# Attention opening and loop ordered by one table for four engines, attention outputs normalised per token

## The chip, the cores and the metric

The kernel runs on one core of one Trainium2 chip. Time is device time in microseconds (us), the median of the runs made. The engines speak of themselves as in the profile: PE is the matrix engine (PEld its weight loads), DVE the vector engine, ACT the scalar engine, POOL GpSimd; SP only issues transfers.

## The reference

Two batches of 768 tokens, 8 heads of 64: attention with 8 global and 96 local keys, then a dense feed-forward layer with a Mish gate over 1536 tokens, then a mixture of 8 experts with one expert per token.

```python
scores = scale * np.matmul(q, k.transpose(0, 1, 3, 2)) + bias      # bias: -slope * distance
a = np.exp(np.where(keep, scores, -1e9) - max)
attn = np.matmul(a / (a.sum(-1) + 1e-9), v)                        # 12 tiles of 128 tokens
h = x @ w_in                                                       # 1536x512 @ 512x2048, float64 weights
x = (h * tanh(softplus(h))) @ w_out                                # 2048x512
expert = argmax(x @ w_gate); out = gate * (relu(x @ w1[expert]) @ w2[expert])
```

## The kernel before

Attention is done tile by tile (12 tiles of 128 tokens), each in two steps of four heads (24 steps `s`). A step is: `a_S` scores on PE into PSUM; `a_max` (DVE, one instruction per head: bias added and row maximum); `a_exp` (ACT, with the row sum); `a_T` transposes of the probabilities on PE; `a_Tev` copies of them to SBUF (ACT); `a_V` the product with v on PE. After both steps of a tile, before the change, `a_recip` inverts the sums and spreads them over 512 columns on DVE (L324), `a_R` transposes that on PE (L330), `a_Rc` copies it to SBUF on ACT (L335), and `a_xm` multiplies the outputs, which stand with features on the partitions, by it. `a_xh` and `a_xl` split the result in a rounded part and a remainder.

The feed-forward layer is cut into 48 units (three passes over the weights, 6 blocks of 256 tokens): per unit `L1_mms` is 24 matmuls of 256 columns (L441), `L2_mms` 12 of 512 columns (L460), two units later; between them stands the Mish chain of 11 parts (0, 2, 3, 4 and 9 on ACT, the others on DVE, L468 to L500). The weights come as 64-bit floats in 32 chunks; each is converted by `next_conv(0)`, three DVE instructions (L168, L170, L172), `next_conv(1)`, one on ACT (L206), and `next_conv(2)`, one on DVE (L208). 16 chunks serve the first two passes, units 0 to 23; the other 16 are first used by unit 24.

The first 10 units (0 to 9) are woven into the attention steps. Only the opening (up to step 4) stands under a manual schedule there; the loop after it is written in Python order, and the framework's scheduler decides where on each engine an instruction stands. It pulled instructions of the code behind the loop, conversions above all, into the loop. What follows the loop, units 10 to 47, the routing and the experts, is written the same in both kernels. Transfers are issued by SP in one order. `prefill` writes zero rows to the gather buffer with 24 transfers, all at unit 16.

In the opening, `fill` issues matmuls of the identity that compute nothing needed; `make_ints` turns the two integer inputs, loaded to all 128 partitions, into floats; the bias tiles `ndist` are built from them on DVE in ten instructions a part (`bias_part`, L113 to L122); `prep_qk` scales a tile's q in one instruction (DVE for tile 0, POOL for the others, L267).

Of the kernel before, what the change touches and what calls it, by code (L numbers as in the profile page):

```python
# [8 lines left out]
F32 = mybir.dt.float32  # L9
# [25 lines left out]
NWARM = 17  # L35
# [7 lines left out]
def moe_kernel(ctx, tc, q, k, v, n_global, n_local, w_in, w_out, w_gate, w1, w2, out, dbg=None):  # L43
# [17 lines left out]
    int_raw = const.tile([128, 2, 2], I32, name="int_raw")  # L61
    for i_, src_ in enumerate((n_local, n_global)):
        nc.scalar.dma_start(int_raw[:, i_, :], src_.bitcast(I32).unsqueeze(0).broadcast_to([128, 2]))
# [4 lines left out]
    def make_ints():  # L68
        f = const.tile([128, 2, 2], F32, name="int_f")
        nc.vector.tensor_copy(f, int_raw)  # L70
        neg = const.tile([128, 2], F32, name="int_n")
        nc.vector.tensor_single_scalar(neg, f[:, :, 0], 0.0, op=ALU.is_lt)
        nc.vector.tensor_add(neg, neg, f[:, :, 1])
        nc.vector.scalar_tensor_tensor(out=nlg, in0=neg, scalar=4294967296.0, in1=f[:, :, 0],
                                       op0=ALU.mult, op1=ALU.add)

# [181 lines left out]
    def prep_qk(t):  # L258
# [6 lines left out]
        eng = nc.vector if t == 0 else nc.gpsimd  # L265
        with tc.issue_after(gorder[0]) if t > 2 else nullcontext():
            eng.tensor_tensor(out=qkt[t], in0=qkt[t], in1=qsc.unsqueeze(2).to_broadcast([128, 4, 128]), op=ALU.mult)  # L267
# [15 lines left out]
    rbs = {}  # L283
# [35 lines left out]
    def a_recip(t):  # L319
        su = rcs.pop(t)  # L320
        nc.vector.tensor_scalar_add(su, su, 1e-9)
        nc.vector.reciprocal(su, su)
        sp_ = xe.tile([128, ROW], F32, tag="x2", name="sp_")[:, 0:DM]
        nc.vector.tensor_copy(sp_.rearrange("p (a b) -> p a b", b=64), su.unsqueeze(2).to_broadcast([128, H, 64]))  # L324
        rbs[t] = sp_

    def a_R(t):
        rb = ps.tile([128, 4, 128], F32, tag="b", name="rb")
        for p_ in range(4):
            nc.tensor.transpose(rb[:, p_, :], rbs[t][:, p_ * 128:p_ * 128 + 128], ident)  # L330
        rbs[t] = rb

    def a_Rc(t):
        rs = xe.tile([128, ROW], F32, tag="x2", name="rs")[:, 0:DM].rearrange("p (a b) -> p a b", a=4)
        nc.scalar.copy(rs, rbs[t])  # L335
        rbs[t] = rs

# [26 lines left out]
    def a_V(s):  # L364
# [4 lines left out]
        if pr == 0:  # L369
            av_ps[t] = ps.tile([128, 4, 128], F32, tag="b", name="av")  # L370
        av = av_ps[t]
        va = vv[0:nk, 0]
        vb = vv[:, 1]
        for i in range(2):
            for c in range(2):
                for j in range(2):
                    q_ = 2 * i + j
                    h = 4 * pr + q_
                    hs = slice(h * 64, h * 64 + 64)
                    lh = va[:, hs] if c == 0 else vb[:, hs]  # L380
                    rh = PT[0:nk, 0, q_, :] if c == 0 else PT[:, 1, q_, :]
                    nc.tensor.matmul(av[64 * j:64 * j + 64, 2 * pr + i, :], lhsT=lh, rhs=rh,
                                     start=(c == 0), stop=(c == 1))
# [3 lines left out]
    def a_xm(t):  # L387
# [4 lines left out]
        xm = rbs.pop(t)  # L392
        nc.vector.tensor_mul(xm, av_ps.pop(t), xm)
        return xm

    def a_xh(t, xm):
        blk, o = divmod(t, 2)
        nc.scalar.copy(xT[blk][0][:, :, o * 128:o * 128 + 128], xm)  # L398

    def a_xl(t, xm):  # L400
# [3 lines left out]
        ins = nc.vector.tensor_sub(xl[:, :, cs], xm, xh[:, :, cs].bitcast(F32)).ins  # L404
# [7 lines left out]
        return ins  # L412

    def a_x(t):
        xm = a_xm(t)
        a_xh(t, xm)
        return a_xl(t, xm)
# [96 lines left out]

    def acc_evac(u):
        p, b, j = units[u]
        ac = accs.pop(b)
        for o in range(2):
# [8 lines left out]
            else:  # L527
                if p == 0:
                    xp = xe.tile([128, DM], F32, tag="xp", name="xpo", bufs=4)
                    nc.scalar.copy(xp, ac[o])  # L530
                else:
                    xp = xpl[b][o]
                    nc.vector.tensor_add(xp, ac[o], xp)
# [76 lines left out]
    def prefill():  # L610
# [9 lines left out]
    pass  # L620
# [233 lines left out]
    NS = 5  # L854
    with tc.manual_schedule(engines={mybir.EngineType.PE, mybir.EngineType.Activation, mybir.EngineType.DVE, mybir.EngineType.Pool}), tc.tile_pool(name="tmp0", bufs=1, side="right") as tmp0:
# [8 lines left out]

        fill(NWARM)
        ci = tmp0.tile([128, NG], I32, name="ci")
# [3 lines left out]
        next_raw()  # L870
        load_v(1)
        load_qk(2)
        next_raw()
        next_raw()
        def some(it, n_):
            for _ in range(n_):
                next(it, None)

        def heads(f, s_, qs=range(4)):
            for q_ in qs:  # L880
                f(s_, q_)
# [8 lines left out]
        make_ints()  # L890
        nc.vector.tensor_scalar(out=gk, in0=cf, scalar1=ng, scalar2=None, op0=ALU.is_lt)
        some(b0, 4)
        prep_qk(0)
        some(b0, 5)
        a_S(0)
        a_S(1)
        prep_qk(1)
        bias_diag(ndist)
        heads(a_max, 0)
        heads(a_exp, 0)  # L900
        heads(a_max, 1)
        some(b1, 11)
        bias_copies(ndist)
        fill(4)
        a_T(0, 0)
        a_T(0, 1)
        heads(a_exp, 1)
        a_S(2)
        a_Tev(0, 0)
        a_Tev(0, 1)  # L910
        a_T(1, 0)
# [529 lines left out]
```

## Time and profile before

| | |
|---|---|
| runs | 603.31, 601.72, 603.13 us; median 603.13 |
| profiled execution | 601.62 us; its span from first to last instruction 599.8 us |
| busy share of the span | PE 96%, PEld 86%, DVE 80%, ACT 63%, POOL 15% |
| granted TensorE clock | 0.996 on average |
| moved by DMA | 109.97 MB, mean 183 GB/s |

Times in the rows below are from the start of the span. The attention part lasts to 156.9 us, where unit 10, the first one behind the loop, starts on PE. A busy time joins the overlapping spans of an engine's instructions: an instruction of 0.69 us can be followed by the next one after 0.60 us, so the distance of two starts is what an instruction costs its engine.

### The profile page before, as it was taken

How to read it: one execution, taken by the hardware profiler on the slowest of the kernel's cores; microseconds unless marked ns; L12 is line 12 of the kernel's file. 1: busy time of each engine (PE TensorE's matmuls, PEld its weight loads, DVE VectorE, ACT ScalarE, POOL GpSimd, SP SyncE). 2: the span in 40 equal slices, each digit the busy share in tenths (PEclk: the TensorE clock that was granted, in tenths of full speed). 3: DMA queues.
4: the chain of work that ended last, by engine and by line, in shares of the span. 5: the costliest groups of instructions: out<-in, count | busy, mean ns of one | idle time of the engine just before them, and what ended most of it. 6: DMA issues, size and time to landing. Idle time of an engine off the chain costs nothing.

```text
span 599.8 us, 11918 instructions
## 1 busy us (share of the span) xinstructions
PE 575.7 (96%) x4288; PEld 518.5 (86%) x4288; DVE 480.0 (80%) x1151; ACT 378.7 (63%) x882; POOL 88.4 (15%) x157
## 2 busy tenths in 40 slices
PE   8988999999999999999999999989999999999994
PEld 7766777777889899898989889779999999999994
DVE  5999999999699899776867667655985678888942
ACT  3898788898676565656455555465664566776731
POOL 3211210000110010010210301121201212113111
PEclk9999999999999999999999999999999999999998
DMA  7976555756899856322221310367667284586200
GB/s 225 343 246 190 179 209 172 241 191 229 282 304 300 326 187 227 113 71 80 98 89 54 106 36 36 114 251 281 203 243 251 96 310 164 199 307 235 106 18 22
DMA packets 54935, 109.97 MB, mean 183 GB/s; under 512 B 5723, under 2 KB 12891, under 8 KB 54866
## 3 DMA queue, kind: packets, MB, share of 16 engines
q1 hardware_dynamic: 48882, 90.21, 45.0%
q0 software_dynamic: 5696, 18.89, 9.6%
q8 instruction: 36, 0.59, 0.4%
q14 instruction: 33, 0.27, 0.1%
q10 hardware_dynamic: 288, 0.00, 0.0%
HBM read 84.67 MB, written 25.10 MB: 183 GB/s over the span
## 4 chain that ended last, share of the span: by engine, by line
PE 66%; DVE 15%; ACT 11%; DMA 5%; issue 2%; SPq 0%; POOL 0%; DVEq 0%; ACTq 0%; POOLq 0%
PE hp L441 18%; PE acc L460 16%; PE bacc L724 6%; PE bhp L724 6%; ACT P L316 3%; PE bacc L725 3%; PE bhp L725 3%; DVE P L305 2%; ACT PT L362 2%; DVE bw L158 2%; PE bhp L727 1%; PE bacc L727 1%; PE bacc L729 1%; PE bacc L728 1%; PE bhp L728 1%
## 5 line engine op out<-in xcount | busy, mean ns | idle before, releaser
L460 PE MATMUL acc<-wpair,gh 128*128 128x512 f32 x384 | 123.8, 400 | 1.4 <-ACT gh L497 1.4
L441 PE MATMUL hp<-xh,wpair 128*128 128x256 f32 x768 | 121.0, 287 | 2.3 <-ACT xh L398 2.2
L441 PEld LDWEIGHTS hp<-xh,wpair 128*128 128x128 f32 x768 | 104.3, 188 | 9.8 <-ACT xh L398 4.2
L460 PEld LDWEIGHTS acc<-wpair,gh 128*128 128x128 f32 x384 | 68.1, 188 | 16.5 <-issue 1.9
L158 DVE TENSOR_TENSOR bw<-bst,bw 128x512 fp32r<-128x512 f32 x112 | 72.9, 685 | 9.7 <-ACT bw L157 8.9
L157 ACT CAST bw<-bst 128x512 fp32r<-128x512 f32 x112 | 64.5, 620 | 19.6 <-PE bhp L728 9.8
L460 PE MATMUL acc<-wpair,gl 128*128 128x512 f32 x192 | 75.4, 393 | 0.8 <-DVE gl L500 0.8
L468 ACT ACTIVATE e<-hp 128x512 f32<-128x512 f32 x48 | 28.7, 598 | 71.3 <-PE hp L441 71.3
L441 PE MATMUL hp<-xl,wpair 128*128 128x256 f32 x384 | 63.9, 284 | 0.3 <-DVE xl L404 0.3
L724 PE MATMUL bhp<-xc,bw 128*128 128x352 f32 (+4 forms) x192 | 59.3, 364 | 0.7 <-DVE t L759 0.6
L724 PE MATMUL bacc<-hc,bw 128*128 128x352 f32 (+4 forms) x192 | 59.2, 364 | 0.0
L316 ACT ACTIVATE P<-P,mx 128x232 f32<-128x232 f32 (+1 forms) x96 | 44.7, 470 | 15.1 <-DVE mx L305 15.0
L441 PEld LDWEIGHTS hp<-xl,wpair 128*128 128x128 f32 x384 | 52.8, 188 | 1.0 <-DVE xl L404 0.9
L725 PE MATMUL bhp<-xc,bw 128*128 128x176 f32 (+4 forms) x192 | 48.5, 253 | 0.0
L725 PE MATMUL bacc<-hc,bw 128*128 128x176 f32 (+4 forms) x192 | 48.3, 252 | 0.0
L478 DVE SCALAR_TENSOR_TENSOR n<-n,r 128x512 f32<-128x512 f32 x48 | 33.1, 689 | 16.7 <-ACT r L476 15.9
L460 PEld LDWEIGHTS acc<-wpair,gl 128*128 128x128 f32 x192 | 36.1, 188 | 8.8 <-DVE gl L500 1.3
L500 DVE SCALAR_TENSOR_TENSOR gl<-n,gh 128x512 fp32r<-128x512 f32 x48 | 33.0, 688 | 11.6 <-ACT gh L497 10.6
L497 ACT ACTIVATE gh<-n 128x512 fp32r<-128x512 f32 x48 | 30.1, 628 | 13.4 <-DVE n L493 13.2
L472 ACT ACTIVATE n<-e 128x512 f32<-128x512 f32 x48 | 30.3, 632 | 13.1 <-DVE e L470 13.0
L724 PEld LDWEIGHTS bhp<-xc,bw 128*128 128x128 f32 x192 | 36.1, 188 | 1.7 <-DVE t L759 0.8
L423 POOL DMA_DIRECT2D xl<-xs x12 | 6.9, 576 | 204.9 <-PE hp L441 137.1
(220 smaller groups left out, 1278.2 us busy)
## 6 DMA issues: line engine op xcount, KB each, us to landing
bst<-in_moe_w_dram SPq DMA_DIRECT2D x56, 512.0 KB
wst<-in_moe_w_in_dram SPq DMA_DIRECT2D x16, 512.0 KB
wst<-in_moe_w_out_dram SPq DMA_DIRECT2D x16, 512.0 KB
xl<-xs POOLq DMA_DIRECT2D x12, 512.0 KB, 4.0
xh<-xs POOLq DMA_DIRECT2D x12, 512.0 KB, 4.9
xpl<-xps SPq DMA_DIRECT2D x24, 256.0 KB
xg<-z SPq DMA_DIRECT2D x24, 224.9 KB
w0f<-in_moe_w_dram SPq DMA_DIRECT2D x8, 512.0 KB
```

The source lines that it names most:

```text
L157: nc.scalar.copy(hi, src)
L158: nc.vector.tensor_sub(lo, src, hi.bitcast(F32))
L316: nc.scalar.activation(out=Ps[s][:, q_, 0:w], in_=Ps[s][:, q_, 0:w], func=AF.Exp, bias=mxs[s][:, q_:q_ + 1], scale=-1.0, accum_out=rcs[t][ ...
L441: yield lambda f=f, kk=kk, wi=wi, xx=xx, cs=cs: nc.tensor.matmul(hp[:, f, :], lhsT=w[:, wi, kk, cs], rhs=xx[:, kk, :], start=(kk == 0 and ...
L460: yield lambda f=f, o=o, cs=cs, gi=gi, wi=wi, first=first, last=last: nc.tensor.matmul(accs[b][o], lhsT=gi[:, cs], rhs=w[:, wi, f, :], sta ...
L468: nc.scalar.activation(out=e, in_=hp, func=AF.Exp, scale=-1.0)
L472: nc.scalar.activation(out=n, in_=e, func=AF.Square)
L478: nc.vector.scalar_tensor_tensor(out=n, in0=n, scalar=0.25, in1=r, op0=ALU.add, op1=ALU.mult)
L497: nc.scalar.mul(gts[u][0], n, -(2.0 ** -80))
L500: nc.vector.scalar_tensor_tensor(out=gl, in0=n, scalar=-(2.0 ** -80), in1=gh.bitcast(F32), op0=ALU.mult, op1=ALU.subtract)
L724: nc.tensor.matmul(o[:, 0:2 * cap], lhsT=wh, rhs=xc, start=first, stop=False)
L725: nc.tensor.matmul(o[:, 0:cap], lhsT=wl, rhs=xh, start=False, stop=last)
```

## The change

Opening and loop now stand in one table, `ORDER`, of 666 operations, all under the manual schedule for PE, ACT, DVE and POOL: each engine runs its instructions in the order of the table. The letters are the functions above (S scores, M maximum, E exponential, T and C transposes and their copies, V product with v, R, N, X, h, l the end of a tile, L and G four matmuls of `L1_mms` and three of `L2_mms`, m a part of the Mish chain, c, d, e the three parts of a conversion, v the copy of a finished partial sum).

`a_V` swaps its operands: the probabilities are the weights, v streams, and the output has tokens on the partitions. Each of the 8 matmuls of 128 columns in a step becomes two of 64. The inverted sums are then one factor per partition and head: one DVE instruction per tile (`a_n`) reads the PSUM output and applies them, four transposes (`a_X`) bring features to the partitions, and `a_xh`, `a_xl` read those from PSUM. The spread, its transposes and its copy fall away. The integers are loaded to one partition and spread by a matmul with ones; q of tiles 0 and 1 is scaled on ACT in eight pieces; 17 and 4 filling matmuls become 6 and 3; the 24 zero-row transfers are spread over units 14 to 21, three each. The Mish chain of unit 9 is finished inside the table.

```diff
-NWARM = 17
+NWARM = 6
+LOOPU = 10
...
-    int_raw = const.tile([128, 2, 2], I32, name="int_raw")
+    int_raw = const.tile([1, 2, 2], I32, name="int_raw")
...
+        nc.tensor.matmul(warm[:, 0:2], lhsT=one, rhs=z, start=True, stop=True)
+        nc.vector.tensor_copy(nlg, warm[:, 0:2])
...
+    def scale_q(s):
+        t, pr = divmod(s, 2)
+        for p_ in (2 * pr, 2 * pr + 1):
+            nc.scalar.mul(qkt[t][:, p_, :], qkt[t][:, p_, :], qsc[:, p_:p_ + 1])
...
-                    nc.tensor.matmul(av[64 * j:64 * j + 64, 2 * pr + i, :], lhsT=lh, rhs=rh,
-                                     start=(c == 0), stop=(c == 1))
+            for c in (1, 0):
+                n = nk if c == 0 else 128
+                for j in range(2):
+                    r = slice(64 * j, 64 * j + 64)
+                    nc.tensor.matmul(av_ps[t][r, h, :], lhsT=PT[0:n, c, q_, r], rhs=vv[0:n, c, h * D:h * D + D],
+                                     start=(c == 1), stop=(c == 0))
...
+    def a_n(t):
+        xns[t] = xe.tile([128, ROW], F32, tag="x2", name="xn")[:, 0:DM]
+        nc.vector.tensor_tensor(out=xns[t].rearrange("p (a b) -> p a b", b=D), in0=av_ps.pop(t),
+                                in1=rcs.pop(t).unsqueeze(2).to_broadcast([128, H, D]), op=ALU.mult)
+
+    def a_X(t):
+        xn = xns.pop(t)
+        xps_[t] = ps.tile([128, 4, 128], F32, tag="b", name="xp")
+        for p_ in range(4):
+            nc.tensor.transpose(xps_[t][:, p_, :], xn[:, p_ * 128:p_ * 128 + 128], ident)
...
+    ORDER = """
+    q0 b0 q1 S0 S1 M0.0 q2 M1.0 M1.1 E0.0 M0.1 S2 M0.2 E1.0 M0.3 M1.2 E0.1 M1.3 b1 E0.2 E0.3 b2 E1.1 T0.0 E1.2 c0
...
+    m9.9 l11 v2.0 G7 v2.1 m10.9 G7 e13 v3.0 v3.1
+    """.split()
...
+        for tok in ORDER:
+            ACT_[tok[0]](*tok[1:].split("."))
...
-        if u == 16:
-            prefill()
+        if 14 <= u < 22:
+            for _ in range(CAPMAX // 112):
+                next(zero_rows, None)
```

On PE, one place in the loop: before, a step's scores (`sp`), transposes (`pt`), the product with v (`av`) and the transposed sums (`rb`).

```order
L292 MATMUL sp<-kT,qr 128x232 x4
L347 MATMUL pt<-ident,P 104x128 x4
L349 MATMUL pt<-ident,P 128x128 x4
L382 MATMUL av<-PT,vv 64x128 x8
L330 MATMUL rb<-ident,sp__566 128x128 x4
```

The same engine now, behind the scores of tile 1 (`xp` is the transposed output of a tile).

```order
L301 MATMUL sp<-kT,qr 128x232 x8
L337 MATMUL pt<-ident,P 104x128 x4
L339 MATMUL pt<-ident,P 128x128 x4
L337 MATMUL pt<-ident,P 104x128 x4
L339 MATMUL pt<-ident,P 128x128 x4
L385 MATMUL xp<-ident,xn 128x128 x4
L367 MATMUL av<-vv,PT 64x64 x32
```

A step's product with v is 16 matmuls of 64 columns where it was 8 of 128 (the 32 are two steps); the four transposes a tile stand on its output in place of its sums.

On DVE, the rows from the remainder of the last tile (`xl`) on, before: 22 conversions (`cv<-wst`) of 32 have been started up to here, eight of them from the code behind the loop.

```order
L404 TENSOR_TENSOR xl<-rs,xh 128x4x128
L482 TENSOR_TENSOR e<-e,r 128x512
L493 TENSOR_TENSOR n<-e,hp 128x512
L500 SCALAR_TENSOR_TENSOR gl<-n,gh 128x512
L470 TENSOR_SCALAR e<-e 128x512
L208 TENSOR_TENSOR wpair_0_2480<-cv,wpair_0_2480 128x512 x2
L168 TENSOR_SCALAR cv<-wst 128x512 x2
L170 SCALAR_TENSOR_TENSOR cv<-wst,cv 128x512
L478 SCALAR_TENSOR_TENSOR n<-n,r 128x512
```

The same place now; the second `gl` row ends the chain of unit 9.

```order
L398 TENSOR_TENSOR xl<-xp,xh 128x4x128
L488 SCALAR_TENSOR_TENSOR gl<-n,gh 128x512
L211 TENSOR_TENSOR wpair_0_1866<-cv,wpair_0_1866 128x512
L173 SCALAR_TENSOR_TENSOR cv<-wst,cv 128x512
L171 TENSOR_SCALAR cv<-wst 128x512
L175 SCALAR_TENSOR_TENSOR cv<-wst,cv 128x512
L173 SCALAR_TENSOR_TENSOR cv<-wst,cv 128x512
L175 SCALAR_TENSOR_TENSOR cv<-wst,cv 128x512
L458 TENSOR_SCALAR e<-e 128x512
L211 TENSOR_TENSOR wpair_2_2290<-cv,wpair_2_2290 128x512
```

The table holds 14 conversions, and the scheduler draws two more ahead of this place, so that 16 have been started here where it was 22 (15 against 22 are through their three instructions, 14 against 20 through the last one). From the `gl` of unit 9 to that of unit 23, the last unit that needs none of the later weights, DVE's order holds 165 instructions on 512 columns, 31 of them with one tensor operand (`TENSOR_SCALAR`), 134 with two.

On SP, the zero rows (`xg<-z`) before, in nearly one piece:

```order
L618 DMA xg<-z 112x514 x9
L534 DMA xps<-xpo 128x512 x2
L512 DMA xpl<-xps 128x512 x2
L618 DMA xg<-z 112x514 x12
L534 DMA xps<-xpo 128x512 x2
L618 DMA xg<-z 112x514
L182 DMA wst<-in_moe_w_in_dram 128x2x512
```

and now:

```order
L614 DMA xg<-z 112x514 x3
L185 DMA wst<-in_moe_w_in_dram 128x2x512
L507 DMA xps<-xpo 128x512 x2
L500 DMA xpl<-xps 128x512 x2
L185 DMA wst<-in_moe_w_in_dram 128x2x512
L190 DMA wst<-in_moe_w_out_dram 128x1024
L507 DMA xps<-xpo 128x512 x2
L614 DMA xg<-z 112x514 x2
```

They stand in groups of at most three; before, four weight chunks (`wst`) stand behind the first of them, now eight.

## Rows read from the trace of the kernel before

**Rows 1.** Windows: busy us of PE, PEld, DVE, ACT, POOL, clock, DMA share, GB/s.

```profile
0.00:10.80 10.80, 8.47 (x54) 8.18 (x55) 5.55 (x28) 1.28 (x1) 3.99 (x26) 1.00 0.68 197
15.00:150.00 135.00, 127.61 (x1072) 101.48 (x1070) 131.60 (x384) 114.47 (x314) 13.82 (x20) 1.00 0.67 222
0.00:156.90 156.90, 146.24 (x1194) 117.15 (x1194) 143.64 (x440) 124.57 (x342) 21.07 (x55) 1.00 0.68 222
156.90:237.30 80.40, 79.56 (x506) 72.03 (x507) 75.38 (x135) 50.31 (x86) 7.76 (x14) 1.00 0.87 272
```

**Rows 2.** The chain that ended last: start us, us, what.

```profile
156.91 0.74 PE hp L441 x4
...
162.83 2.88 PE hp L441 x24
165.71 2.76 PE acc L460 x12
...
245.86 2.76 PE acc L460 x12
```

**Rows 3.** Timeline of the opening: start us, us, engine, line, instruction, wait before it.

```profile
1.67 6.89 PE L863 MATMUL warm<-ident 128*128 128x128 f32 x34 [1.67 <-POOL ident masks.py:199]
...
6.74 0.17 DVE L70 CAST int_f<-int_raw 128x4 f32<-128x4 int32 x1 [3.61 <-DMA int_raw<-in_n_global_dram]
...
8.44 0.68 DVE L267 TENSOR_TENSOR qr<-qr,qsc 128x512 f32<-128x512 f32 x1
...
8.76 1.26 POOL L267 TENSOR_TENSOR qr<-qr,qsc 128x512 f32<-128x512 f32 x1 [3.24 <-DMA qr<-in_q_dram]
9.04 1.07 DVE L119 TENSOR_SCALAR loc<-loc 128x136 f32<-128x136 f32 x1
...
10.81 0.30 DVE L305 CUSTOM_DVE_ANT_0 P<-sp,ndist 128x136 f32<-128x136 f32 x1 [0.15 <-DVE ndist L122]
...
13.30 0.21 DVE L119 TENSOR_SCALAR loc<-loc 128x104 f32<-128x104 f32 x1
```

**Rows 4.** Timeline of PE inside the loop.

```profile
124.73 1.05 PE L292 MATMUL sp<-kT,qr 64*128 64x232 f32 x8
125.71 0.74 PE L460 MATMUL acc<-wpair,gh 128*128 128x512 f32 x2
...
126.52 0.60 PE L347 MATMUL pt<-ident,P 128*104 128x128 f32 x4
126.96 0.60 PE L349 MATMUL pt<-ident,P 128*128 128x128 f32 x4
...
128.32 0.60 PE L330 MATMUL rb<-ident,sp__1685 128*128 128x128 f32 x4
128.85 1.10 PE L382 MATMUL av<-PT,vv 104*64 104x128 f32 x16
129.88 0.50 PE L460 MATMUL acc<-wpair,gh 128*128 128x512 f32 x1
```

**Rows 5.** Windows of line L382 alone: busy of PE and PEld.

```profile
0.00:156.90 156.90, 28.62 (x384) 20.33 (x384) 1.00 0.68 222
```

**Rows 6.** The chain again, the routing's logits.

```profile
277.63 1.04 PE lp L555 x32
```

**Rows 7.** Windows of line L324 alone: busy of DVE.

```profile
0.00:156.90 156.90, 6.13 (x12) 1.00 0.68 222
```

**Rows 8.** Timeline of DVE behind the loop.

```profile
188.01 0.69 DVE L208 TENSOR_TENSOR wpair<-cv,wpair 128x512 fp32r<-128x512 f32 x1
188.61 0.69 DVE L482 TENSOR_TENSOR e<-e,r 128x512 f32<-128x512 f32 x1
189.22 0.42 DVE L470 TENSOR_SCALAR e<-e 128x512 f32<-128x512 f32 x1
189.55 0.69 DVE L493 TENSOR_TENSOR n<-e,hp 128x512 f32<-128x512 f32 x1
```

**Rows 9.** Waits, 160 to 215 us: who waited for what, us in total, times, longest.

```profile
DVE cv L168 <- DMA wst<-in_moe_w_in_dram: 1.7, 1, 1.7
```

More of the change, by code (lines that the diff above doesn't have):

```diff
@@ L317, in a_exp @@
                              bias=mxs[s][:, q_:q_ + 1], scale=-1.0, accum_out=rcs[t][:, h:h + 1])
[L319 to L336, printed above, removed]
     pts = {}
@@ L513, in part_load, with evac0 @@
             xpl[b].append(xp)
+    def evac0(b, o):
+        t = 2 * b + o
+        xp = xe.tile([128, DM], F32, tag="xp", name="xpo", bufs=4)
+        nc.scalar.copy(xp, accs[b][o])
+        nc.sync.dma_start(xps[t * 128:(t + 1) * 128, :], xp)
+        if o == 1:
+            del accs[b]
     def acc_evac(u):
         p, b, j = units[u]
+        if p == 0:
+            evac0(b, 0)
+            evac0(b, 1)
+            return
         ac = accs.pop(b)
@@ L527, in acc_evac @@
             else:
[L528 to L533, printed above, removed]
+                xp = xpl[b][o]
+                nc.vector.tensor_add(xp, ac[o], xp)
                 nc.sync.dma_start(xps[t * 128:(t + 1) * 128, :], xp)
@@ L618, in prefill @@
                 tc.keep_in_program_order(nc.sync.dma_start(xg[r0:r0 + 112, :], z))
-    pass
+                yield
+    zero_rows = prefill()
     cnt = const.tile([1, NE], F32, name="cnt")
@@ L865, in moe_kernel @@
         fill(NWARM)
+        wi = ps.tile([128, 512], F32, tag="b", name="wi")
+        one = tmp0.tile([128, 128], F32, name="one")
+        z = tmp0.tile([128, 2], F32, name="z")
+        nc.vector.memset(one, 1.0)
+        nc.vector.memset(z, 0.0)
         ci = tmp0.tile([128, NG], I32, name="ci")
@@ L889, in moe_kernel @@
         some(b1, 2)
-        make_ints()
+        make_ints(z, one, wi)
+        fill(3)
         nc.vector.tensor_scalar(out=gk, in0=cf, scalar1=ng, scalar2=None, op0=ALU.is_lt)
-        some(b0, 4)
         prep_qk(0)
[L894 to L906, printed above, removed]
@@ L1050, in moe_kernel, with bias, v_end, scores @@
-    u0 = u
+        def bias(part):
+            some({"0": b0, "1": b1, "2": b1}[part], 4 if part == "1" else 11)
+            if part == "0":
+                bias_diag(ndist)
+            if part == "2":
+                bias_copies(ndist)
+        l1 = [L1_mms(u) for u in range(LOOPU)]
+        l2 = [L2_mms(u) for u in range(LOOPU)]
+        def v_end(s):
+            a_V(s)
+            if s % 2 and s // 2 + 2 < NTILE:
+                load_v(s // 2 + 2)
+        def scores(s):
+            a_S(s)
+            if s % 4 == 3 and 1 < s // 2 // 2 + 2 + 0 < NTILE // 2 and s > 3:
+                load_qk(2 * (s // 4) + 4)
@@ new lines, in half1, with consts @@
+        def half1(c):
+            next_conv(0)
+            next_raw()
+        def consts(_):
+            make_fast()
+            build_consts(tmp0)
+        ACT_ = {
+            "b": lambda a: bias(a), "q": lambda s: scale_q(int(s)), "p": lambda t: prep_qk(int(t)),
+            "S": lambda s: scores(int(s)), "V": lambda s: v_end(int(s)), "R": lambda t: a_rec(int(t)),
+            "N": lambda t: a_n(int(t)), "X": lambda t: a_X(int(t)), "h": lambda t: a_xh(int(t)),
+            "l": lambda t: a_xl(int(t)), "c": half1, "d": lambda c: next_conv(1), "e": lambda c: next_conv(2),
+            "k": consts,
+            "M": lambda s, q_: a_max(int(s), int(q_)), "E": lambda s, q_: a_exp(int(s), int(q_)),
+            "T": lambda s, c: a_T(int(s), int(c)), "C": lambda s, c: a_Tev(int(s), int(c)),
+            "L": lambda u: run_mms(l1[int(u)], 4), "G": lambda u: run_mms(l2[int(u)], 3),
+            "m": lambda n, u: mish(int(u), int(n)), "v": lambda b, o: evac0(int(b), int(o)),
+        }
@@ L1079, in phase_, with chain @@
         run_mms(it, 99)
+    def chain(u, *parts):
+        if 0 <= u < NU:
+            for q_ in parts:
+                mish(u, q_)
     for u in range(u0, NU + 2):
@@ L1110, in moe_kernel @@
             next_conv(1)
-        chain(u - 1, 10)
+        chain(prev, 10)
         for _ in range(nch):
```

233 lines of the change are left out of this document (52 added, 181 removed).

## The prediction

> **What bounds the kernel now.** I read the windows first. Inside the loop (15 to 150 us) DVE is busy 131.60 of 135 us, 97%, ACT 114.47 (85%), PE 127.61 [rows 1]. PE's 95% deceives, because the end of a matmul is modelled: a distance of starts says more. Its timeline gives 0.98 us for a score step (124.73 to 125.71), 0.44 for four transposes (126.52 to 126.96), 1.03 for a product with v (128.85 to 129.88), 0.53 for the four transposes of the sums (128.32 to 128.85) [rows 4]; the chain gives 2.88 us for an L1 and 2.76 for an L2 [rows 2]. So PE's need up to unit 10 is 24 x (0.98 + 2 x 0.44 + 1.03) = 69.4, 12 x 0.53 = 6.4, 10 x 2.88 = 28.8 and 8 x 2.76 = 22.1: 126.7 us. It had from the end of the filling matmuls at 8.56 [rows 3] to 156.91 [rows 2], 148.3 us, and was really at work for 85%. DVE bounds the attention part, and PE waits for it in small pieces.
>
> Behind the loop PE is the bound: from 156.91, where unit 10's L1 starts, to 245.86, where unit 23's L2 starts [rows 2], stand 16 L1 and 15 L2, 16 x 2.88 + 15 x 2.76 = 87.5 us of work in 88.95. But DVE has little left there too: 75.38 of 80.40 us [rows 1].
>
> **The change, part by part.**
>
> *Sums applied per token, DVE.* The 12 spreads vanish: 6.13 us [rows 7]. The multiplication stays one instruction per tile with a PSUM operand, and so does `xl`; I cost both as before (0.60 us from start to start [rows 8]). No row shows an operand that is repeated 64 times from one column; if it ran twice as long, the price is 12 x 0.6 = 7 us of DVE.
>
> *PE.* The transposes change places, 12 x 4 before and after. The product with v keeps its streamed columns but doubles the weight loads, to 32 per step in the trace's count (16 instructions, two passes each). The nearest row is the routing's logits: 32 matmuls with 64 weight columns each, in two halves of the array, 1.04 us [rows 6], against 1.03 for today's product. They stream only 8 columns, so this bounds from below: it shows that such loads follow each other at 0.033 us. From above: today's loads are busy 20.33 us for 384 [rows 5], 0.053 us each; if these stand one behind the other, a step takes 32 x 0.053 = 1.69 us, and PE gains 24 x 0.66 = 15.8 us. I take the lower value, since the logits have the same shape of weights and the same alternation of halves. The Trainium skill (TensorE: Matmul & The Clock Gate, section "LDWEIGHTS (loading the stationary operand)") speaks against the change here: a load costs its columns divided by 1.2 ns, 53 ns for 64 columns, 1.71 us a step. By that PE's need would be 143 us instead of 126.7; the logits' row does not bear it out for alternating halves.
>
> *Conversions leave the loop.* At the last `xl` DVE has 14 two-operand instructions and 6 one-operand ones of conversions fewer, and 6 of their subtractions: 20 x 0.60 + 6 x 0.33 = 14.0 us [rows 8]. With the spreads, the q scaling (0.68 [rows 3]) and two chain instructions more (1.2), DVE's 143.64 us up to 156.9 [rows 1] become about 143.6 - 14.0 - 6.1 - 0.7 + 1.2 = 124. ACT loses 12 copies and some conversions and gains eight short scalings; it stays under its 124.57 us. So three engines now need 124, under 124 and 126.7 us: PE, by a little, is the one that the table has to keep busy.
>
> *Opening.* The first maximum stands at 10.81 us. DVE waits 3.61 us for the integers, to 6.74; then the scaling of q, 0.68, stands in its way, and L119 takes 1.07 us while POOL's own scaling runs from 8.76, where the narrower one at 13.30 takes 0.21 [rows 3]. Both scalings leave: about 1.5 us earlier. One descriptor for each integer in place of 128 should come earlier, the matmul and copy behind it cost something; no row shows either: I bound it by -1 and +2 us and take +1. Together 2.5 us, so the table starts at 8.3 and PE's scores at about 8.2. Tile 1's q lands only at 8.76 [rows 3], and ACT's first exponential now stands behind its scaling, which holds ACT's part of the gain to about 2 us.
>
> *Fewer filling matmuls.* The granted clock is shown as 1.00 for 0 to 10.8 us [rows 1], but 34 matmuls of 128 columns took 6.89 us, 0.20 each [rows 3], where the loop's 128-column transposes take 0.11 [rows 4]: most of them ran at the lower level of 1.2 GHz, and PE was busy without a break until the speed doubled. With 12 of them, a wait, and 8 more, the rise may come later; if it comes 6 us later, with PE busy half that time, 3 us are lost, partly under DVE's and ACT's first work. I take 1.5 us, between 0 and 5. By the Trainium skill (the same page, Part 1, "The HAM clock gate") the lower level is the default and only activity lifts it, which bears in the same direction.
>
> *Where unit 10 starts.* DVE as the bound of the old loop reached 97% [rows 1]. I give PE the same: 8.2 + 126.7 / 0.97 + 1.5 = 140.3 us, against 156.9. With no wait at all it is 134.9; at 93%, 145.9.
>
> *What is given back behind the loop.* DVE's order from unit 9's `gl` to unit 23's has 165 instructions: 134 x 0.60 + 31 x 0.33 = 90.6 us, with 2% for waits 92.5, against PE's 87.5. DVE starts on it about 1 us ahead of unit 10's L1. So DVE becomes the bound there, and unit 23's L2 starts 91.5 us after unit 10's L1, at 231.8, where it was 245.86. Past it DVE has no conversions left, and the instructions are the same in both kernels: the 14.1 us stay to the end. Spreading the zero rows moves no byte away; eight weight chunks now stand among them on SP's queue where four did. One such wait cost 1.7 us before [rows 9]; I count none, and price it as a rival.
>
> *The sum.* 601.62 - 14.1 = 587.5 for a run like the profiled one, which lies 1.5 us below the median of the three; I predict 588 us.
>
> **The rivals.**
> 1. Better: the table runs without waits, the clock rises as early as before, and DVE's 90.6 us behind the loop are hidden to the last 2 us: unit 10 at 135, unit 23's L2 at 135 + 89.5 = 224.5, 21 us gained, 580. For it: in its best stretch behind the loop PE was busy 79.56 of 80.40 [rows 1]. Against it: three engines that are all filled above 90% and each held to a fixed order wait for each other.
> 2. Weight loads that don't overlap: PE needs 142.5 us, unit 10 at 8.2 + 142.5 / 0.97 + 1.5 = 156.6, no sooner than before, and DVE's 91.5 then end at 248: 604, slower by 2. It decides when a step of `av` passes about 1.6 us.
> 3. The order itself stalls, and this ends on the slower side: an instruction at the head of one engine's queue waits for a value that the table's author expected earlier, and everything behind it on that engine waits as well, which the old loop's scheduler avoided by pulling other work forward. If PE is at work for no more than 85%, as now, unit 10 starts at 8.2 + 149.1 + 1.5 = 158.8, and with the longer DVE list behind it unit 23's L2 at 250.3, 4.4 us late: 606. It decides at 88%: there nothing is gained.
> 4. Weights late: from 156.9 to 237.3 the DMA share was 0.87 at 272 GB/s [rows 1], and the same bytes plus four chunks must pass in less time. Three waits of the size of the one seen cost 5 us: 592.
>
> **How the numbers follow.** The forecast, 588 with 583 to 592 as its own range (PE at 95 to 99% of its time in the table), has a chance of 0.48; rival 1 0.14, rival 2 0.08, rival 3 0.12, rival 4 0.18. The range of 578 to 599 takes in the forecast, rivals 1 and 4, and leaves out 2 and 3, two in ten. A difference of 0.3%, 1.8 us, is about what a measurement of this kernel can tell from none. Faster by more than that hold the forecast, rivals 1 and 4 and the milder cases of 3: 0.83; the same 0.06; slower 0.11.
>
> **What would show it.** In the profile after: the first maximum at 8 to 9 us; a step of `av` with 32 matmuls at 1.0 to 1.1 us from start to start; no L324, L335; DVE under 95% and PE's real work over 93% up to unit 10's L1, which starts at 136 to 145 us; from there to unit 23's L2 90 to 94 us, with PE waiting for `gl` and DVE nearly full. It would be wrong if `av` costs 1.6 us or more, if the stretch behind the loop keeps 88 us, or if the loop shows waits of PE on ACT or DVE that add up to more than 15 us.

## The result, and the profile after

The changed kernel took 586.71 us (median of four runs, 586.55 to 590.01); the kernel before, on the same chip, 603.22 us (601.72 to 606.16). The ratio is 0.9733, with a 95% interval of 0.9683 to 0.9784: 16.5 us faster. The profiled execution took 586.55 us, with a span of 584.8 us where it had been 599.8.

The page after, engines' busy time in the whole span:

```profile
span 584.8 us, 12654 instructions
PE 563.5 (96%) x4650; PEld 519.9 (89%) x4650; DVE 471.6 (81%) x1141; ACT 374.2 (64%) x878; POOL 84.6 (14%) x156
```

PE shows 96% as before. Where the time went is seen only by stage. The windows after, with the columns of [rows 1]:

```profile
0.00:138.40 138.40, 132.02 (x1556) 117.77 (x1557) 124.94 (x407) 116.85 (x331) 18.89 (x54) 0.99 0.70 222
15.40:18.80 3.40, 3.40 (x42) 2.68 (x40) 2.20 (x13) 1.76 (x7) 1.83 (x2) 0.50 1.07 377
138.40:230.50 92.10, 89.38 (x572) 80.64 (x571) 91.70 (x166) 58.47 (x100) 7.79 (x14) 1.00 0.92 298
```

Up to unit 10, DVE has 124.94 us of work in 138.40, where it had 143.64 in 156.90 [rows 1]. Behind the loop it is DVE that is full, 91.70 of 92.10 us. The chain that ended last after, which answers to [rows 2], gives the two marks:

```profile
22.76 2.01 PE av L367 x64
...
135.83 2.75 PE acc L448 x12
138.57 2.88 PE hp L429 x24
...
223.94 1.19 PE acc L448 x4
225.13 0.72 PE hp L429 x6
225.85 1.85 PE acc L448 x8
227.70 3.00 PE hp L429 x25
230.70 0.92 PE acc L448 x4
```

Unit 10's L1 starts at 138.57 us instead of 156.91: 18.3 us earlier. Unit 23's L2 starts at about 230.6 instead of 245.86: 15.2 us earlier, so 3 us are given back between the two. From there on nothing changes; the span is 15.0 us shorter.

The opening after, the timeline that answers to [rows 3]:

```profile
1.67 2.93 PE L890 MATMUL warm<-ident 128*128 128x128 f32 x12 [1.67 <-POOL ident masks.py:199]
...
3.83 0.19 DVE L71 CAST int_f<-int_raw 1x4 f32<-1x4 int32 x1 [0.70 <-DMA int_raw<-in_n_global_dram]
...
5.14 0.93 PE L890 MATMUL warm<-ident 128*128 128x128 f32 x6
5.32 0.16 DVE L78 COPY nlg<-wi 128x2 f32<-128x2 f32 x1 [0.68 <-PE wi L77]
...
6.00 1.20 PE L301 MATMUL sp<-kT,qr 64*128 64x136 f32 x16
...
7.39 0.30 DVE L314 CUSTOM_DVE_ANT_0 P<-sp,ndist 128x136 f32<-128x136 f32 x1 [0.15 <-PE sp L301]
...
14.05 1.03 PE L367 MATMUL av<-vv,PT 72*64 72x64 f32 x28 [1.40 <-DMA vv<-in_v_dram]
15.02 1.56 PE L301 MATMUL sp<-kT,qr 64*128 64x232 f32 x8
16.50 1.97 PE L367 MATMUL av<-vv,PT 128*64 128x64 f32 x32
```

The integers land 2.9 us earlier (3.83 against 6.74), the first maximum stands at 7.39 instead of 10.81. The last row is a step of `av` at the lower clock (granted 0.50 from 15.40 to 18.80): it takes 1.97 us there, and the chain above shows two of them in 2.01 us later.

### The profile page after: what moved, and what is told of

The parts are those of the page before. It is cut to its first block, busy times and chain, and to the rows that moved or that the text cites. A ratio compares the mean times of both kernels' runs of the same rounds, so it can differ in the third digit from the quotient of the medians.

```text
span 584.8 us, 12654 instructions
## 1 busy us (share of the span) xinstructions
PE 563.5 (96%) x4650; PEld 519.9 (89%) x4650; DVE 471.6 (81%) x1141; ACT 374.2 (64%) x878; POOL 84.6 (14%) x156
## 4 chain that ended last, share of the span: by engine, by line
PE 77%; DVE 11%; DMA 4%; issue 3%; ACT 2%; SPq 1%; POOL 1%; DVEq 0%; POOLq 0%; ACTq 0%
PE hp L429 19%; PE acc L448 19%; PE bacc L721 6%; PE bhp L721 6%; PE av L367 3%; PE bacc L722 3%; PE bhp L722 3%; PE sp L301 3%; PE bhp L724 1%; PE bacc L724 1%; PE bacc L726 1%; PE bhp L725 1%; PE bacc L725 1%; PE bhp L726 1%; DMA xg<-x,dsi 1%
## 5 line engine op out<-in xcount | busy, mean ns | idle before, releaser
L448 PE MATMUL acc<-wpair,gh 128*128 128x512 f32 x384 | 120.7, 398 | 4.2 <-ACT gh L485 4.2
L429 PE MATMUL hp<-xh,wpair 128*128 128x256 f32 x768 | 118.4, 285 | 0.0
L429 PE MATMUL hp<-xl,wpair 128*128 128x256 f32 x384 | 62.0, 282 | 0.0
L721 PEld LDWEIGHTS bhp<-xc,bw 128*128 128x128 f32 x192 | 36.1, 188 | 1.7 <-DVE t L756 0.8
L722 PEld LDWEIGHTS bhp<-xc,bw 128*128 128x128 f32 x192 | 36.7, 191 | 0.0
L722 PEld LDWEIGHTS bacc<-hc,bw 128*128 128x128 f32 x192 | 36.7, 191 | 0.0
```

What stands on the lines that cost most here:

```text
L429: yield lambda f=f, kk=kk, wi=wi, xx=xx, cs=cs: nc.tensor.matmul(hp[:, f, :], lhsT=w[:, wi, kk, cs], rhs=xx[:, kk, :], start=(kk == 0 and ...
L448: yield lambda f=f, o=o, cs=cs, gi=gi, wi=wi, first=first, last=last: nc.tensor.matmul(accs[b][o], lhsT=gi[:, cs], rhs=w[:, wi, f, :], sta ...
L721: nc.tensor.matmul(o[:, 0:2 * cap], lhsT=wh, rhs=xc, start=first, stop=False)
L722: nc.tensor.matmul(o[:, 0:cap], lhsT=wl, rhs=xh, start=False, stop=last)
```

## The experiments

Each ratio is to the kernel before on the same chip, with its 95% interval. "Unit 10" is the start of its L1, "stretch" the time from there to unit 23's L2. Marks are read from the one profiled execution of each kernel, in PE's timeline, which starts a block up to 0.2 us ahead of the chain's piece: the changed kernel's unit 10 stands at 138.41 there and at 138.57 in the chain. The experiments ran on three chips, on which the kernel before took 603.6 to 605.0 us where it took 603.2 beside the changed kernel; so small differences between experiments are given by the ratios too.

**1. One conversion per unit.** The later conversions were issued two in every third unit and one in the others.

```diff
-        nch = (1 + (u % 3 == 0)) if u < 30 else 0
+        nch = 1 if u < 30 else 0
```

> The changed kernel with one conversion per unit behind the loop (units 10 to 27) in place of 1, 1, 2: DVE's list from unit 9's gl to unit 23's then holds 154 instructions of 512 columns (29 and 125) in place of 165, 85.0 us in place of 91.1. If DVE binds that stretch (my theory), it falls from 92.1 us to PE's 87.5 to 89, and the time to about 583.5 us. If it is the transfers among the zero rows or PE itself that make 92 us of 87.5, nothing moves: 586 to 587 us.

582.92 us, ratio 0.9638 (0.9607 to 0.9668), below the changed kernel's interval, so this version beats both. Its window behind the loop:

```profile
138.70:226.30 87.60, 87.60 (x566) 79.92 (x565) 87.18 (x158) 55.65 (x96) 7.38 (x14) 1.00 1.00 316
```

Unit 10 stays (138.67 against 138.41). The stretch falls from 92.1 to 87.6 us, and PE is busy in all of it, with 566 matmuls where the longer stretch had 572. DVE's instructions here are 158 where they were 166; the missing ones were only moved past unit 23, into units that have time for them. The same edit moves the loads of the raw weight chunks, but in the changed kernel no wait of DVE for a transfer shows between 138.4 and 230.5 us. So what the changed kernel gave back was DVE's list, as predicted. PE's work alone, predicted at 87.5 us, is now reached.

**2. Zero rows in one burst.** The 24 transfers at unit 16 again, as before the change.

```diff
-        if 14 <= u < 22:
-            for _ in range(CAPMAX // 112):
-                next(zero_rows, None)
+        if u == 16:
+            for _ in zero_rows:
+                pass
```

> The changed kernel with all 24 zero-row transfers at unit 16 again. My theory (DVE binds behind the loop, transfers are hidden): the same time within 1.5 us, 585.5 to 588.5, with a wait of a conversion on its weights of up to 3 us in the trace. Rival (the spread of the zero rows is a good part of the gain): 590 us or more.

592.91 us, ratio 0.9798 (0.9766 to 0.9830). By the medians it is 6.2 us slower than the changed kernel, by the ratios, whose intervals overlap, 3.9; the spans of the two profiled executions differ by 3.4 (588.2 against 584.8). The theory of the expectation, the same time within 1.5 us, was missed. Waits from 138 to 245 us (us in total, times, longest), of this kernel:

```profile
PE acc L448 <- ACT gh L485: 5.4, 2, 3.3
DVE cv L171 <- DMA wst<-in_moe_w_out_dram: 3.9, 1, 3.9
```

and its window:

```profile
138.70:235.00 96.30, 90.79 (x572) 81.83 (x572) 91.93 (x166) 58.50 (x100) 7.51 (x14) 0.98 0.89 285
```

DVE does the same 91.9 us of work in 4.2 us more: the one wait of 3.9 us for a weight chunk that stands behind the zero rows. DVE was already the bound, so nothing takes the wait up. PE then waits in its turn for what DVE is late with. Spreading the zero rows is worth about 4 us of the 16.5, and 6 at most.

**3. The table without the fixed order.** All operations in the table's order of writing, but outside the manual schedule, so that the scheduler decides.

```diff
-        for tok in ORDER:
-            ACT_[tok[0]](*tok[1:].split("."))
+    for tok in ORDER:
+        ACT_[tok[0]](*tok[1:].split("."))
```

> The changed kernel with the table's operations issued in the table's order, but outside the manual schedule, so that the framework's scheduler decides each engine's order and pulls conversions into the loop again (22 in place of 16 started at the last xl). If the fixed order matters (theory): unit 10 starts later, at 145 to 152 us, DVE is over 95% busy in the loop, and half of that comes back behind the loop, where PE is the bound again: 589 to 595 us. If the gain is that of the removed DVE work and of the opening alone: within 2 us of the changed kernel, 585 to 589 us.

602.84 us, ratio 0.9968 (0.9946 to 0.9990): nearly the whole gain is gone, more than either expectation had. But part of it is lost at the very start. DVE's timeline:

```profile
10.65 0.69 DVE L175 SCALAR_TENSOR_TENSOR cv<-wst,cv 128x512 int32<-128x512 int32 x1
...
16.71 0.30 DVE L314 CUSTOM_DVE_ANT_0 P<-sp,ndist 128x136 f32<-128x136 f32 x1 [0.38 <-PE sp L301]
```

The scheduler put conversions ahead of the bias, and the first maximum stands at 16.7 us. So the run does not tell what the order does in the loop; experiment 7 was made for that.

**4. Only the new outputs, in the old kernel.** The old loop, opening and scheduler, with the new `a_V`, `a_n`, `a_X` at the old places.

```diff
     def a_x(t):
-        xm = a_xm(t)
-        a_xh(t, xm)
-        return a_xl(t, xm)
+        a_n(t)
+        a_X(t)
+        a_xh(t)
+        return a_xl(t)
...
-            if s % 2 == 0:
-                a_R(s // 2 - 1)
-                a_Rc(s // 2 - 1)
             a_V(s - 1)
```

> The kernel before with only the sums applied per tile and the swapped product with v (no spread, no copy of the transposed sums, twice the weight loads), in the old loop under the scheduler. Theory: the old loop is bound by DVE, which loses 12 x 0.42 to 0.51 = 5 to 6 us of 144, so unit 10 starts 4 to 6 us earlier and the time is 597 to 599.5 us. Rival (the restructuring of the output is most of the gain): 592 us or less. If the longer chain from v to x (DVE, PE, ACT, DVE) is exposed in this order: 602 us or more.

612.33 us, ratio 1.0109 (1.0071 to 1.0147): slower, by some 7 us, though DVE has less to do (no spreads). The theory of the expectation, a gain of 4 to 6 us, was missed; its last case, the longer chain exposed, is what came. Waits from 15 to 140 us, and the window from the first maximum to unit 10:

```profile
PE av L359 <- ACT PT L344: 8.5, 8, 3.4
ACT xh L384 <- PE xp L377: 5.9, 5, 2.3
DVE xn L370 <- PE av L359: 3.5, 2, 2.5
```

```profile
10.80:167.00 156.20, 141.60 (x1528) 116.21 (x1526) 134.17 (x401) 119.64 (x329) 17.33 (x30) 0.96 0.64 209
```

The spread, transposed sums and their copy could be made while the product with v was still to come. Now the product, the multiplication, the transposes and the copy follow each other: PE, DVE, PE, ACT, DVE, and each waits for the one ahead; the first of these waits was 1.9 us in the kernel before. Unit 10 starts at 167.0 us. Behind such waits the granted clock fell too: it was at 0.50 for 6.8 us from 38.1 and again from 55.2, PE was busy for 11.7 us of these, and so up to 5.8 us of PE's time went to the clock. How the 7 us divide between the longer chain and the slower clock behind its waits, the run does not show.

**5. The table with the old outputs.** The opening and table as in the change, but the old `a_V` and the spread, with R as the old `a_recip`, X as the old `a_R`, and h as copy, multiplication and `xh` in one place.

```diff
+        a_Rc(t)
+        xm = rbs.pop(t)
+        nc.vector.tensor_mul(xm, av_ps.pop(t), xm)
...
-            "N": lambda t: a_n(int(t)), "X": lambda t: a_X(int(t)), "h": lambda t: a_xh(int(t)),
+            "N": lambda t: None, "X": lambda t: a_R(int(t)), "h": lambda t: a_xh(int(t)),
```

> The changed kernel with its table, but the old end of a tile: sums spread on DVE, transposed, copied on ACT, outputs with features on the partitions (8 matmuls of 128 columns a step). DVE gets 12 x 0.34 to 0.43 = 4 to 5 us more, ACT 12 x 0.47 = 5.6 us, PE nothing. If PE binds in the table (my forecast's reading), most of that is hidden and unit 10 starts 1 to 4 us later: 588 to 591 us. If DVE or ACT are as tight as PE, all of it shows: 592 to 594 us. If the normalisation were the source of the gain: 600 us or more.

603.11 us, ratio 1.0007 (0.9976 to 1.0037): no gain is left, where 588 to 591 us were expected. Unit 10 starts at 154.1 us. Waits from 15 to 160 us:

```profile
ACT xh L406 <- DVE rs L404: 11.4, 12, 1.7
DVE rs L404 <- ACT rs L394: 6.5, 8, 1.7
```

Copy, multiplication and rounding stand in one place of the table, and each waits for the one before, once per tile. These stalls belong to the way the old outputs were put into a table made for others; experiment 9 pulls them apart.

**6. The old loop in its own order.** The old kernel, with its loop wrapped in a manual schedule, so that each engine follows the Python code.

```diff
-    while s <= NST:
...
+    with tc.manual_schedule(engines={mybir.EngineType.PE, mybir.EngineType.Activation, mybir.EngineType.DVE, mybir.EngineType.Pool}):
+        while s <= NST:
```

> The kernel before with its loop also under the manual schedule, in the order in which its Python code stands: the eight conversions from behind the loop can't enter it (16 started at the last xl, as in the changed kernel), and behind the loop DVE has 162 instructions, 89.5 us. If what counts is that DVE is relieved in the loop, unit 10 starts earlier, at 140 to 150 us, and the time is 590 to 598. If the interleaving of the table counts (theory), the coarse order stalls: unit 10 at 158 us or later, and with the longer DVE list behind it 606 us or more.

631.53 us, ratio 1.0479 (1.0439 to 1.0520). Its windows:

```profile
9.20:169.50 160.30, 142.95 (x1156) 114.11 (x1153) 123.18 (x378) 120.19 (x330) 18.19 (x31) 0.96 0.54 176
169.50:275.60 106.10, 92.45 (x572) 82.38 (x573) 98.54 (x178) 61.98 (x104) 7.38 (x14) 0.95 0.85 269
```

DVE was 97% busy in the old loop [rows 1]; in this fixed order it is at 123.18 of 160.30, 77%, and the conversions that no longer find a place in the loop make the stretch behind it 106.1 us. This fixed order costs 28 us; what matters is which order. Part of it is the clock behind the waits: it was granted at 0.96 and 0.95 in the two windows, at 0.50 for 23.9 us in all, for 18.2 of which PE was busy.

**7. The fixed order for the opening alone.** The table up to its first L0 (130 operations) stays in the manual schedule, the rest of it goes to the scheduler.

```diff
-        for tok in ORDER:
+        SPLIT = ORDER.index("L0")
+        for tok in ORDER[:SPLIT]:
             ACT_[tok[0]](*tok[1:].split("."))
+
+    for tok in ORDER[SPLIT:]:
+        ACT_[tok[0]](*tok[1:].split("."))
```

> The changed kernel with the first 130 operations of the table (up to the first L1 matmuls) under the manual schedule, and the rest left to the scheduler, which again draws conversions into the loop (22 started at the last xl). The opening then stays as in the changed kernel, first maximum at 7.3 us, unlike in the run with everything free, where conversions stood ahead of the bias. Theory: the loop alone, from the first maximum to unit 10, takes 131 us in the table's order and about 142 free; half comes back behind the loop: unit 10 at 148 to 151 us, PE bound behind it, 592 to 595 us. Rival (the opening was all that was lost): unit 10 at 138 to 141 us, 582 to 586.

591.49 us, ratio 0.9803 (0.9768 to 0.9839). Its windows, and its first maximum:

```profile
8.30:147.50 139.20, 130.53 (x1536) 115.70 (x1535) 131.91 (x397) 118.05 (x332) 15.87 (x25) 0.99 0.75 240
147.50:235.10 87.60, 87.60 (x566) 79.88 (x565) 79.41 (x140) 54.04 (x92) 7.38 (x14) 1.00 0.84 264
```

```profile
9.18 0.30 DVE L314 CUSTOM_DVE_ANT_0 P<-sp,ndist 128x136 f32<-128x136 f32 x1 [0.69 <-PE sp L301]
```

Left free, the scheduler pulls 22 conversions into the loop, as in the kernel before, and DVE is at 131.91 of 139.20 us, 95%. The opening did not stay as it was: short instructions of later code came in between, and the first maximum stands 1.8 us later than in the changed kernel (9.18 against 7.39), where it was expected to stay. Unit 10 starts 9.2 us later, but the conversions done early make the stretch 87.6 us, and 4.5 come back. Leaving the loop to the scheduler costs 4.8 us at the end by the medians (591.49 against 586.71) and 4.2 by the ratios, whose intervals overlap a little; how much of it is the later opening is not shown. So the fixed order of the loop is worth about 4 to 5 us at most, and the rest of the gain does not need it.

**8. Experiment 1 with v loaded earlier.** The second weight chunk's load stands behind that of the second v, since PE waits for v in the opening.

```diff
-        next_raw()
         load_v(1)
+        next_raw()
```

> The version with one conversion per unit, with the second weight chunk loaded behind tile 1's v. In the changed kernel PE waited 1.4 us for v at 14 us, and the granted clock then stood at the lower level from 15.4 to 18.8 us. If that wait goes, 1 to 2.5 us: 580.5 to 582 us against 582.9. If the second chunk is then late for its conversion, or tile 2's q is what is waited for next: no change, 582 to 584.

582.63 us, ratio 0.9653 (0.9624 to 0.9682): no difference from experiment 1 (0.9638). PE waited for v for 2.0 us in this profile against 0.2 in that of experiment 1 and 1.4 in the changed kernel, so the move of one load did not bring v earlier, and the wait did not show in the time.

**9. Experiment 5 with the stages apart.** The copy (Z) and the multiplication (Y) get places of their own, at one and two thirds of the way from X to h in the table.

```diff
+            "N": lambda t: None, "Z": lambda t: a_Rc(int(t)), "Y": lambda t: a_mul(int(t)), "X": lambda t: a_R(int(t)), "h": lambda t: a_xh(int(t)),
...
+        for t in range(NTILE):
+            x, h = ORDER.index(f"X{t}"), ORDER.index(f"h{t}")
+            ORDER.insert(x + 1 + (h - x) * 2 // 3, f"Y{t}")
+            ORDER.insert(x + 1 + (h - x) // 3, f"Z{t}")
```

> The old end of a tile inside the table once more, but its two additional steps (ACT's copy of the transposed sums, DVE's multiplication) get places of their own between the transposes and the split, so that ACT and DVE don't wait for each other at one place, as they did 12 times in the run before it. If that run lost its 16 us by those waits, this one starts unit 10 at 142 to 149 us and takes 591 to 596 us: the price of the work itself (DVE 12 x 0.4, ACT 12 x 0.47). If the added work itself costs so much, unit 10 stays at 153 to 155 and the time at 601 to 604 us.

600.91 us, ratio 0.9957 (0.9925 to 0.9988). Waits from 8 to 154 us, and the window of the loop:

```profile
ACT xh L406 <- DVE rs L399: 8.1, 10, 2.4
DVE rs L399 <- ACT rs L394: 7.6, 8, 1.7
```

```profile
7.00:153.30 146.30, 130.93 (x1137) 111.14 (x1137) 128.00 (x389) 120.62 (x337) 17.54 (x30) 0.99 0.61 197
```

The 591 to 596 us hoped for were missed: the waits hardly shrank, and unit 10 stays at 153.3. No engine is full (PE 89%, DVE 87%, ACT 82%), which speaks for the order as what still binds; it is argued and not shown. How much of the distance to the changed kernel a table made for the old outputs could win stays open; 12 spreads and 12 copies more are work that it would have to place.

**10. Experiment 1 with the burst of experiment 2.** Both edits. If the slack that experiment 1 gives DVE takes up a late chunk, the burst should cost little.

> One conversion per unit behind the loop, and all 24 zero-row transfers at unit 16. The burst cost 6 us in the changed kernel, where a conversion waited 3.9 us for its weights while DVE had no slack. With DVE's list 2.5 us shorter than PE's, part of such a wait should be absorbed: 584 to 587 us. If the burst hurts by itself (late reloads of x, or PE waiting for something else), the cost stays: 588 us or more.

593.15 us, ratio 0.9826 (0.9783 to 0.9869): the burst costs 10 us here, more than alone. Waits from 170 to 240 us, then the stretch and a part of it:

```profile
DVE cv L171 <- DMA wst<-in_moe_w_in_dram: 7.8, 1, 7.8
PE acc L448 <- DVE gl L488: 7.0, 1, 7.0
```

```profile
139.20:235.40 96.20, 89.15 (x565) 80.86 (x564) 87.41 (x157) 55.68 (x96) 7.39 (x14) 0.96 0.91 288
196.78:203.61 6.83, 3.03 (x7) 2.45 (x8) 5.31 (x10) 1.48 (x3) 0.00 (x0) 0.50 1.06 400
```

The expectation was missed. An engine that follows one order stops as a whole: the conversion at its head waits 7.8 us for the chunk, behind it in DVE's order stands a `gl`, and PE waits 7.0 us for it. During this wait the granted clock fell to 0.50 and stayed there for 6.8 us, so that PE's work in the stretch takes 1.55 us more (89.15 against 87.60). Wait and clock together are the 8.6 us by which the stretch is longer than in experiment 1. Slack of DVE elsewhere in the stretch doesn't help against one wait of this length.

**11. The integers to 128 partitions again.** Load and arithmetic as before the change, without the matmul.

```diff
-    int_raw = const.tile([1, 2, 2], I32, name="int_raw")
+    int_raw = const.tile([128, 2, 2], I32, name="int_raw")
...
-        nc.tensor.matmul(warm[:, 0:2], lhsT=one, rhs=z, start=True, stop=True)
-        nc.vector.tensor_copy(nlg, warm[:, 0:2])
```

> The changed kernel with the two integers loaded to 128 partitions again, without the matmul and the copy that spread them. They landed at 6.7 us before and at 3.8 now; the table then starts about 2 us later, but tile 1's q, which ACT waits for, lands at 7.5 us in either case. If the start of the table carries through: 588 to 589 us. If ACT's wait for q hides it: 586.5 to 587.5 us.

588.86 us, ratio 0.9744 (0.9709 to 0.9780). DVE's timeline has the integers where they were before the change:

```profile
6.37 0.17 DVE L71 CAST int_f<-int_raw 128x4 f32<-128x4 int32 x1 [3.24 <-DMA int_raw<-in_n_global_dram]
```

The first maximum stands at 9.04 us, later than in each of the four kernels that share the changed opening (7.39, and 7.97, 7.24 and 7.13 in experiments 1, 2 and 10). Unit 10 starts at 140.31, 1.9 us later than with the change, but in this trace PE also waited 2.25 us at the start of the scores and the granted clock was at 0.50 for 3.4 us from 8.4 on, so these 1.9 us are not the integers' alone. The medians differ by 2.1 us and the intervals overlap; the effect is shown for the first maximum, not for the time.

**12. The longer first filling.** NWARM = 17 instead of 6; the second group of filling matmuls stays at 3.

> The changed kernel with 17 filling matmuls in place of 6 at the start. PE is then busy with them until 4.7 us or later, and the matmul that spreads the integers, and the scores, stand behind them: 0 to 2 us later. If the shorter filling was the risk that I priced at 1.5 us, the clock rises earlier and nothing is lost: 585 to 587 us. If the filling is only in the way: 587 to 589 us.

588.04 us, ratio 0.9735 (0.9696 to 0.9775). PE's and DVE's rows of the opening:

```profile
1.67 5.81 PE L890 MATMUL warm<-ident 128*128 128x128 f32 x34 [1.67 <-POOL ident masks.py:199]
...
7.64 0.16 DVE L78 COPY nlg<-wi 128x2 f32<-128x2 f32 x1 [3.02 <-PE wi L77]
...
9.70 0.30 DVE L314 CUSTOM_DVE_ANT_0 P<-sp,ndist 128x136 f32<-128x136 f32 x1 [0.15 <-DVE ndist L125]
```

The matmul that spreads the integers now stands behind the filling, and DVE waits 3.02 us for it. The first maximum comes 2.3 us later, unit 10 at 139.30, 0.9 later; the time can't be told from the changed kernel's. The clock gained nothing by the longer filling that the end shows.

## Why the prediction was right

Forecast 588 us, measured 586.71; the gain was put at 14.1 us, and the span is 15.0 shorter. The forecast's own mechanism is what the runs show, with the opening off, and one term put at nothing that was worth something. At unit 10 the sum lies 1.7 us off: the start came 2.2 us earlier than costed, and PE's waits and the clock together took 5.9 us where 5.4 were allowed. That the 5.4 came so near is partly luck, since what they stood for, a late rise of the clock, did not happen in this trace, and a later dip of it did.

**PE could be kept busy up to unit 10.** Predicted at 140.3 us, measured 138.57. PE's need of 126.7 us, from the first score at 6.00, fills 96% of the 132.6 us from there to unit 10; 97% and 1.5 us for the clock were assumed, with 85% before. The start was the term that was off most: PE's scores were put at 8.2 and begin at 6.00.

**A step of `av`.** Costed at 1.03 us on the strength of the logits' row [rows 6], measured 1.00 (two in 2.01, in the chain). The window of its line alone, from 22.7 us on, answers to [rows 5]:

```profile
22.70:138.40 115.70, 22.94 (x704) 21.45 (x704) 1.00 0.65 208
```

704 loads in 21.45 us of weight-load time are 0.030 us each, where those of the old product, of 64 columns too but each beside 128 streamed columns, had shown 0.053. At the granted clock of 0.50 the same step took 1.97 us, 0.062 us a load. By the Trainium skill (TensorE: Matmul & The Clock Gate, section "LDWEIGHTS (loading the stationary operand)") a load takes its columns divided by 1.2 ns, an estimate of 53 ns for 64 columns; at the upper clock this trace does not agree with it as the distance from load to load. Whether the alternation of the loads between the two halves of the array has a part in it, on which the prediction chose, no run tests. Rival 2, which rested on loads in sequence, is refuted: it needed steps of 1.6 us.

**DVE's relief.** Predicted about 124 us up to unit 10, measured 124.94. The factor that one column repeats 64 times, for which the upper bound was 7 us, costs nothing more. DVE's group of `a_n`, busy us and mean ns, stands beside that of `xl`, which has no repeated operand:

```profile
L378 DVE TENSOR_TENSOR xn<-av,su 128x512 f32<-128x512 f32 x12 | 8.2, 685 | 0.6 <-PE av L367 0.5
L398 DVE TENSOR_TENSOR xl<-xp,xh 128x512 fp32r<-128x512 f32 x12 | 8.2, 685 | 0.2 <-ACT xh L392 0.2
```

**The opening.** Predicted 2.5 us earlier, measured 3.4 (10.81 to 7.39). The integers were taken at 1 us of gain, between -1 and 2; experiment 11 puts them at 1.6 for the first maximum against the changed kernel's trace, and between 1.1 and 1.9 against all four with this opening. The rest, 1.8, answers to the 1.5 of the scalings, which no run takes alone.

**The clock.** Taken at a loss of 1.5 us, because fewer filling matmuls might let it rise late. In the changed kernel's trace the last six filling matmuls take 0.93 us from 5.14 on, about 0.15 each against 0.24 for the first twelve (2.93 us), so there the clock rose early; later it was granted at 0.50 from 15.4 to 18.8. Experiment 1 runs the same program up to unit 10, and in its trace it was the other way round: the clock shows 1.00 in those 3.4 us, but it had risen late.

```profile
5.10 1.63 PE L890 MATMUL warm<-ident 128*128 128x128 f32 x6
...
7.97 0.30 DVE L314 CUSTOM_DVE_ANT_0 P<-sp,ndist 128x136 f32<-128x136 f32 x1 [0.78 <-PE sp L301]
```

Its six filling matmuls take 0.27 us each, DVE waits 0.78 us for the scores, and the first maximum comes 0.6 us later; unit 10 starts 0.3 us later. So the late rise that was feared does happen, in some executions (in experiment 8 the six take 1.63 us too), and in this pair it costs 0.6 us at the first maximum, where 1.5 were taken. What the dip of the changed kernel costs by itself can't be read from this pair.

**What is given back.** Predicted a stretch of 91.5 us, bound by DVE's list; measured 92.1, with DVE busy for 91.70. Experiment 1 shows it to be the list, and not PE: with 11 instructions fewer in DVE's list, PE's own 87.6 us remain.

**Zero rows.** "I count none" was right for the changed kernel: the largest wait of DVE for a chunk is gone, where it had been 1.7 us [rows 9]. But the prediction gave the spreading no worth, since it moves no byte away. Experiment 2 shows that the burst would have cost about 4 us, 6 at most, near rival 4's price of 5: spreading is what held rival 4 off. This is a term of the change that was costed at nothing and is worth about a quarter of the gain.

**What the terms hid.** The prediction added the edits up as if each kept its worth. Experiments 4, 5 and 9 show that they do not. The new outputs alone, with the old loop's places, lose 1.1%; the table with the old outputs gains nothing to 0.4%; together, 2.7%. The outputs shorten DVE's work but lengthen the chain behind the product with v, and the table puts other work into that chain. Rival 3, stalls by the order, is what experiments 5, 6 and 9 point to, in orders that do not fit the work; the change's own table fits it. Seen in steps from the other side: opening, outputs, spread zero rows and the order of writing bring 603 to 591.5 us (experiment 7, whose opening is 1.8 us late), the loop's fixed order brings 586.7, evened conversions 582.9. The new opening alone, in the old loop, was not run, so its worth at the end is not shown.

## What to carry to other kernels

Count each engine's real need in a stage before and after (distances of starts, not PE's busy share), and ask which engine is the bound in the stage behind it: work taken out of a full stage comes back in the next one, and shows there as a price or, placed where that engine has time, as nothing. A fixed order pays where it fits the chain of the work and costs more than a scheduler where it doesn't, so a shorter operation and the order around it must be tried together. On an engine that follows one order a single late transfer stops everything behind it, so keep long bursts off the queue that feeds it, however idle the engine is on average.

## What the runs showed of the hardware that was not expected

- Weight loads of 64 columns, alternating between two halves of the array, followed each other at 0.030 us at the upper clock (0.053 was what the old product showed with half as many loads, so that figure was no floor), and twice as many loads cost no time: a step took 1.00 us where it had been 1.03.
- The granted clock fell to the lower level, 0.50, for 3.4 us soon after PE had waited 1.40 us for v at 14 us. In experiment 8 PE waited 1.03 us for v at the same product, in experiment 1 only 0.25, and in both the clock stayed at 1.00. The length of the wait alone does not decide it: of the two waits below, the first (changed kernel) left the clock at 1.00, and behind the second (experiment 11) it was at 0.50 for 3.4 us from 226.9 on. What decides stays open.

```profile
223.94 1.19 PE L448 MATMUL acc<-wpair,gh 128*128 128x512 f32 x4 [2.10 <-ACT gh L485]
225.84 1.21 PE L446 MATMUL acc<-wpair,gh 128*128 128x512 f32 x4 [2.08 <-ACT gh L483]
```

- One burst of 24 transfers of 112 x 514 values made DVE wait 3.9 us for a weight chunk behind it in experiment 2 and 7.8 us in experiment 10, although the DMA share of the stretch (0.89 and 0.91) was lower than in experiment 1, where it was 1.00 at 316 GB/s and PE waited for nothing.
